# Strided keys and queries loaded as 72 dense rows, values and reordered weight rows by one transfer per head

## The chip, the cores and the metric

The kernel runs on one core of a Trainium2 chip. The metric is the device time of one execution in microseconds (us), from the first instruction to the last with what lies around them; the profile also gives the span between the first and the last instruction. Lower is better.

## The reference

Eight batches of eight heads of attention (sequence 576, head width 64) feed a mixing step and a feed-forward block. Heads 0 to 3 attend locally (the last 32 positions), heads 4 to 7 attend to positions that are a multiple of 32 away. All weights arrive as 64-bit floats and are turned into pairs of 32-bit parts on the chip.

```python
rel = pos[:, None] - pos[None, :]
mask_local = (rel >= 0) & (rel < 32)
mask_strided = (rel >= 0) & (pos[None, :] % 32 == pos[:, None] % 32)
attn = softmax(where(mask[h], q @ k.T / sqrt(64), -1e9))   # local for h < 4, strided for h >= 4
x = (attn @ v).transpose(0, 2, 1, 3).reshape(8, 576, 512)
u = x + (x.transpose(0, 2, 1) @ U @ V).transpose(0, 2, 1)
out = u + maximum(u @ w_ch1, 0) @ w_ch2                    # w_ch1 512 x 2048, w_ch2 2048 x 512
```

## The kernel before

The feed-forward block is the bulk of the work: 18 blocks of 256 rows, each with 16 column chunks of 128, each chunk a first product (`gemm1`, L781) and a second one (`gemm2`, L798) in pairs of 32-bit parts. Blocks 0 and 1 lead and are interleaved. Before them stands a prefix: the attention of batch 0, the mixing of its result, and the start of the attention of batch 1. The attention of batches 2 to 7 is worked in small steps between the products of earlier blocks.

For batches 0 and 1 the strided heads are done by `early_strided`. A row of 2048 elements (8 KB) of one head holds 32 positions of 64 elements; a head has 18 such rows (`NCH`). Keys and queries are loaded in two halves of 1024 elements (4 KB) into the four `kq` tiles, values into `sv`. The access pattern `wide` takes four heads, 32 rows each, which is 14 rows more than a head has: those rows are of the next head and no one uses them. TensorE transposes each half in eight pieces of 128 columns (L354), ScalarE copies the 18 used columns of each 32 out of PSUM (L356), and the scores are small products by head (L367). The values are the moving side of the products at L401.

The 32 weight chunks of 512 KB are loaded by `load_weights` (L158). For `w1` the chunks t = 2 and 3 take their rows in another order, four groups of 32 rows that lie 64 rows apart, again with one access pattern whose outer dimension is 4. Each chunk is then converted by ScalarE, VectorE and GpSimd (`to_f32`, L112 to L117, L182, L183). Some chunk buffers serve the prefix first (`late`): the `kq` tiles sit in the buffers of chunks 28 to 31.

Nearly all transfers are issued by SyncE (SP in the profile) in one order; the first queries go by ScalarE's queue (L93). The order around the change in the prefix is: `kq` and local loads `xn` of the first pair of heads, `sv`, `xn` of the second pair, `U` and `V`, ten weight chunks, values `vt` of the first local pair (L269 reads them), `kq` of batch 1, two weight chunks, `vt` of the second pair, more chunks, `sv` of batch 1, the rest of the chunks, then `xn` of batch 1 (L298 transposes them). A planner that simulates the program's time sets the final order of instructions on each engine.

Of the kernel before, what the change touches and what calls it, by code (L numbers as in the profile page):

```python
# [11 lines left out]
I64 = mybir.dt.int64  # L12
# [26 lines left out]
def fused_kernel(ctx, tc, q, k, v, U, V, w1_in, w2_in, masks, eye, out):  # L39
    nc = tc.nc  # L40
    B, H, S, D = q.shape
    DM, FF = w1_in.shape
    R = U.shape[1]
    NCH = S // 32
# [5 lines left out]
    const = ctx.enter_context(tc.tile_pool(name="const", bufs=1))  # L50
# [11 lines left out]
    def big(shape, name, dtype=F32):  # L62
        return ap_.tile(shape, dtype, name=name, tag="big")
# [22 lines left out]
    def bank(width):  # L86
        return psx1() if width == 1 else psx2().rearrange("p a x -> p (a x)")
# [3 lines left out]
    def dma(out, in_, eng=None):  # L91
        if eng is not None:
            eng.dma_start(out=out, in_=in_)  # L93
        else:
            last_dma[0] = nc.sync.dma_start(out=out, in_=in_).ins  # L95

    ident = const.tile([128, 128], F32, name="ident")
# [4 lines left out]
    raws, w_parts = {}, {}  # L102
# [48 lines left out]
    def load_weights():  # L151
        for i, g, t in chunks:
            src = w2_in[512 * g + 128 * t:512 * g + 128 * t + 128, :] if i else \
                w1_in[128 * t:128 * t + 128, 512 * g:512 * g + 512] if t < 2 else \
                bass.AP(w1_in.tensor, w1_in[256 + 32 * (t - 2):, 512 * g:512 * g + 512].offset, [[64 * FF, 4], [FF, 32], [1, 512]])
            raws[i, g, t] = const.tile([128, 512], I64, name=f"raw{i}_{g}_{t}", tag=f"w{i}_{g}_{t}")
            with tc.issue_after(last_dma[0]):
                nc.sync.dma_start(out=raws[i, g, t], in_=src)  # L158
            yield

    wl = {"gen": load_weights(), "n": 0}

    def late(x, shape, name, dtype=F32):

        i, g, t = chunks[x]
        return const.tile(shape, dtype, name=name, tag=f"w{i}_{g}_{t}")
# [164 lines left out]
    def early_strided(b, eng=None):  # L331


        tb = 64 * (b % 2)
        def wide(src, n, a):

            return bass.AP(src.tensor, src[b, 4:5].offset + a, [[S * D, 4], [32 * D, 32], [1, n]])

        kq = [[late(28 + 2 * x + y, [128, 1024], "kq") for y in range(2)] for x in range(2)]
        for half in range(2):  # L340
            for bufs, src, e in zip(kq, (k, q), (None, eng)):
                dma(out=bufs[half], in_=wide(src, 1024, 1024 * half), eng=e)
        yield
        sv = big([128, 2 * NCH * D], "sv")[:, 0:32 * D]
        dma(out=sv, in_=wide(v, 32 * D, 0))
        yield
        width = 1 if banks["prefix"] else 2
        kT, qT = [[att([128, 4 * 8 * NCH], "xT") for _ in range(2)] for _ in range(2)]
        for half in range(2):
            for bufs, xT in zip(kq, (kT, qT)):  # L350
                for j0 in range(0, 8, 4 * width):
                    tp = bank(width)
                    for j in range(4 * width):
                        nc.tensor.transpose(out=tp[:, 128 * j:128 * j + 128], in_=bufs[half][:, 128 * (j0 + j):128 * (j0 + j) + 128],  # L354
                                            identity=ident)
                    nc.scalar.copy(out=xT[half].rearrange("p (x i) -> p x i", i=NCH)[:, 4 * j0:4 * j0 + 16 * width],  # L356
                                   in_=tp.rearrange("p (x i) -> p x i", i=32)[:, :, 0:NCH])
                    yield
        sp = psx2()
        for par in range(2):  # L360
# [2 lines left out]
        for j in range(16):  # L363
            for h in range(4):
                c0 = (4 * (j % 8) + h) * NCH
# [29 lines left out]
        for r0 in range(0, 32, 2 * nj):  # L395
            op = bank(width)
            for x in range(2 * nj):
                r = r0 + x
# [6 lines left out]
            half, r1 = r0 // 16, r0 % 16  # L405
# [4 lines left out]
            if r1 + 2 * nj == 16:  # L410
                dma(out=od.rearrange("h i r d -> (h i) r d")[:, 16 * half:16 * half + 16], in_=o_sb[half])
                if b == 0:
                    xT_str.append(late(23 + half, [128, 16, 2, 32], "xT_str"))
                    for y in range(2):
                        nc.vector.transpose(out=xT_str[half].rearrange("p r d i -> p (r d i)")[:, 512 * y:512 * y + 512],
                                            in_=o_sb[half].rearrange("p r d -> p (r d)")[:, 512 * y:512 * y + 512])
# [282 lines left out]
    def attention(b):  # L699
        if b >= NSP:  # L700
            yield from local_pairs(b)
            yield "strided"
            yield from strided_copies(b)
            yield from mixed(b, (0, 1))
        else:
            strided = early_strided(b)
            next(strided)
            yield
            yield from run_staggered([strided] + [early_local(b, pr) for pr in range(2)], LAGB)
            yield "free"  # L710
            yield from mixed(b, (0, 1))
# [133 lines left out]
    n0, c0 = wl["n"], counts["conv"]  # L845
# [5 lines left out]
    for step, (n, fc) in enumerate(seq):  # L851
# [15 lines left out]
        if nb < B and step >= window[nb][0]:  # L867
# [5 lines left out]
            while done < want:  # L873
                done += 1
                r = next(gen, "end")
# [66 lines left out]
```

## Time and profile before

| what | value |
|---|---|
| median of 3 runs | 1135.38 us (1133.37 to 1137.88) |
| the profiled execution, its own time | 1131.09 us |
| its span | 1128.9 us |
| TensorE busy, share of the span | 979.8 us, 87% |
| VectorE, GpSimd, ScalarE busy | 612.0, 359.2, 274.0 us |
| chain that ended last: PE, DMA, SP's queue, VectorE | 77%, 10%, 5%, 5% |
| bytes moved by all transfers | 75.21 MB |

The page gives busy time by engine, the span in 40 slices, the transfers, and the chain of work that ended last, followed back from the last instruction. Further views list an engine's instructions in order of time with the idle time before each and what ended it, and sum a stretch of the span: busy time of each engine, the TensorE clock that was granted, the share of the 16 DMA engines that was busy, and the rate. A DMA share of 0.25 is as much as four of the sixteen engines without a pause.

### The profile page before, as it was taken

The numbers are of one execution on the slowest core, as the hardware profiler recorded it, in microseconds if no ns is written. First come the engines' busy times: TensorE is split into PE (matmuls) and PEld (weight loads), VectorE is DVE, ScalarE is ACT, GpSimd is POOL, SyncE is SP. The second block draws the span as 40 slices with busy tenths as digits, with TensorE's granted clock in tenths as the row PEclk, the third lists the DMA queues.
The fourth block names the chain that finished last, engine by engine and source line by source line (L and its number), as shares of the span: only waits on it lengthen the run. The fifth ranks groups of instructions, "written<-read, shape, count | busy, mean of one in ns | idle before, by whom it ended". The sixth has DMA issues, their size and how long they took to land.

```text
span 1128.9 us, 22425 instructions
## 1 busy us (share of the span) xinstructions
PE 979.8 (87%) x9325; PEld 851.4 (75%) x9325; DVE 612.0 (54%) x1151; ACT 274.0 (24%) x638; POOL 359.2 (32%) x384
## 2 busy tenths in 40 slices
PE   1422752995989999999999999999999999999998
PEld 1311652783878888889888888888888888899997
DVE  0145162944688586747527587678658673322111
ACT  0221041531215121411114222421322242111110
POOL 1013020411764545254403545294427430000000
PEclk9755585995989999999999999999999999999999
DMA  3563655203232423231312423324340410111000
GB/s 104 142 148 113 186 159 152 59 4 91 50 96 45 82 53 68 53 51 49 51 40 41 82 54 68 64 39 83 59 82 15 95 33 20 26 31 38 1 19 19
DMA packets 183433, 75.21 MB, mean 67 GB/s; under 512 B 157084, under 2 KB 172732, under 8 KB 183076
## 3 DMA queue, kind: packets, MB, share of 16 engines
q1 hardware_dynamic: 181868, 72.44, 28.4%
q8 instruction: 73, 1.20, 0.5%
q10 hardware_dynamic: 1464, 1.34, 0.4%
q14 instruction: 28, 0.23, 0.1%
HBM read 54.27 MB, written 11.61 MB: 58 GB/s over the span
## 4 chain that ended last, share of the span: by engine, by line
PE 77%; DMA 10%; SPq 5%; DVE 5%; issue 2%; ACT 1%; POOL 1%; DVEq 0%; POOLq 0%; ACTq 0%
PE ph L781 35%; PE acc L798 32%; SPq L95 5%; DMA xn<-in_k_dram 3%; DMA raw<-in_moe_w_ch_dram 3%; DMA vt<-in_v_dram 2%; DMA kq<-in_q_dram 2%; PE px L798 2%; PE px L237 1%; PE px L269 1%; PE px L257 1%; PE ph L584 1%; DVE st L518 1%; PE px L630 1%; PE px L547 1%
## 5 line engine op out<-in xcount | busy, mean ns | idle before, releaser
L781 PE MATMUL ph<-uh,w 128*128 128x256 f32 x2304 | 470.3, 287 | 5.4 <-ACT w L182 2.1
L781 PEld LDWEIGHTS ph<-uh,w 128*128 128x128 f32 x2304 | 378.1, 191 | 20.2 <-DVE gl L786 2.6
L798 PE MATMUL acc<-w,gh 128*128 128x512 f32 x1088 | 349.4, 400 | 0.8 <-ACT gh L785 0.8
L781 PE MATMUL ph<-ul,w 128*128 128x256 f32 x1152 | 328.1, 285 | 2.1 <-DVE ul L750 1.8
L786 DVE SCALAR_TENSOR_TENSOR gl<-ph,gh 128x256 fp32r<-128x256 f32 x288 | 120.9, 420 | 288.8 <-ACT gh L785 287.7
L785 ACT ACTIVATE gh<-ph 128x256 fp32r<-128x256 f32 x288 | 110.2, 383 | 512.8 <-PE ph L781 457.9
L781 PEld LDWEIGHTS ph<-ul,w 128*128 128x128 f32 x1152 | 220.2, 191 | 13.1 <-DVE ul L750 2.1
L798 PEld LDWEIGHTS acc<-w,gh 128*128 128x128 f32 x1088 | 193.3, 188 | 34.7 <-ACT gh L785 1.2
L798 PE MATMUL acc<-w,gl 128*128 128x512 f32 x544 | 215.6, 396 | 0.0
L488 POOL TENSOR_TENSOR tmp<-st 128x576 f32<-128x576 f32 (+6 forms) x162 | 169.3, 1081 | 123.8 <-DMA vt<-in_v_dram 104.1
L516 POOL TENSOR_TENSOR tmp<-st,s_st 128x448 f32<-128x448 f32 (+7 forms) x162 | 137.1, 876 | 203.9 <-DVE st L518 80.8
L518 DVE TENSOR_REDUCE st<-tmp 128x64 f32<-128x64 f32 (+8 forms) x162 | 136.4, 868 | 2.5 <-POOL tmp L516 1.7
L798 PEld LDWEIGHTS acc<-w,gl 128*128 128x128 f32 x544 | 102.2, 188 | 20.3
L183 POOL TENSOR_TENSOR w<-cv,w 128x512 fp32r<-128x512 f32 x32 | 45.4, 1424 | 192.2 <-ACT w L182 188.0
L490 DVE TENSOR_REDUCE s_st<-tmp 128x9 f32<-128x576 f32 (+6 forms) x162 | 87.5, 563 | 19.6 <-POOL tmp L488 19.5
L269 PE MATMUL px<-vt,PT 64*32 64x65 f32 x1152 | 18.3, 241 | 34.1 <-DMA vt<-in_v_dram 33.3
L298 PE MATMUL px<-ident,xn 128*128 128x128 f32 (+1 forms) x40 | 8.9, 353 | 41.0 <-DMA xn<-in_k_dram 41.0
L269 PEld LDWEIGHTS px<-vt,PT 64*32 64x32 f32 x1152 | 14.6, 113 | 39.7 <-issue 37.2
L533 ACT COPY xg<-st 32x256 f32<-32x256 f32 x96 | 38.7, 404 | 22.9 <-DVE st L518 21.9
L298 PEld LDWEIGHTS px<-ident,xn 128*128 128x128 f32 (+1 forms) x40 | 6.7, 187 | 43.6 <-issue 43.2
L644 DVE TENSOR_TENSOR xg<-px,xg 128x512 f32<-128x512 f32 x32 | 20.4, 683 | 30.7 <-PE px L633 28.4
L114 DVE TENSOR_SCALAR cv<-cv 128x512 int32<-128x512 int32 (+3 forms) x35 | 20.1, 577 | 25.5 <-ACT cv L112 25.1
(135 smaller groups left out, 676.3 us busy)
## 6 DMA issues: line engine op xcount, KB each, us to landing
raw<-in_moe_w_ch_dram SPq DMA_DIRECT2D x32, 512.0 KB
out_dram<-xg SPq DMA_DIRECT2D x32, 256.0 KB
u<-bt SPq DMA_DIRECT2D x240, 32.0 KB
vt<-in_v_dram SPq DMA_DIRECT2D x32, 144.0 KB
vt<-in_v_dram SPq DMA_DIRECT2D x32, 136.0 KB
st<-in_q_dram SPq DMA_DIRECT2D x24, 144.0 KB
st<-in_k_dram SPq DMA_DIRECT2D x24, 144.0 KB
st<-in_v_dram SPq DMA_DIRECT2D x24, 144.0 KB
```

Of the source, the lines that this page charges most:

```text
L95: last_dma[0] = nc.sync.dma_start(out=out, in_=in_).ins
L183: nc.gpsimd.tensor_tensor(out=lo, in0=f, in1=hi.bitcast(F32), op=ALU.subtract)
L269: nc.tensor.matmul(op[32 * o4:32 * o4 + 32, hh, (D + 1) * t:(D + 1) * t + D + 1], PT[rows, 32 * c:32 * c + 32], vt[rows, c], start=True, s ...
L488: nc.gpsimd.tensor_tensor(out=tmp[:, 0:n], in0=sk[:, j0:j0 + n], in1=sq[:, i:i + 1].broadcast_to([128, n, D]), op=ALU.mult)
L490: late.append(lambda tmp=tmp, n=n, i=i, j0=j0: nc.vector.tensor_reduce(out=s_st[:, i, j0:j0 + n], in_=tmp[:, 0:n], axis=AX.X, op=ALU.add))
L516: nc.gpsimd.tensor_tensor(out=tv, in0=sv[:, 0:i + 1, d0:d0 + step], in1=s_st[:, i, 0:i + 1].broadcast_to([128, i + 1, step]), op=ALU.mult)
L518: late.append(lambda tv=tv, i=i, d0=d0, step=step: nc.vector.tensor_reduce(out=o_st[:, i, d0:d0 + step], in_=tv.rearrange("p j d -> p d j" ...
L533: nc.scalar.copy(out=xg[32 * i4:32 * i4 + 32, :, cs], in_=o_st[rows, i4:16:4, :])
L781: nc.tensor.matmul(ph[:, 0:W], w_parts[0, g, dc][:, part, fs], ut[:, :, :, dc, :], start=(dc == 0 and i == 0), stop=(dc == NDC - 1 and i = ...
L785: gate[:] = [nc.scalar.activation(out=gh[:, 0:W], in_=ph[:, 0:W], func=AF.Relu).ins]
L786: nc.vector.scalar_tensor_tensor(out=gl[:, 0:W], in0=ph[:, 0:W], scalar=0.0, in1=gh[:, 0:W].bitcast(F32), op0=ALU.max, op1=ALU.subtract)
L798: nc.tensor.matmul(accs[n][:, s, :], gt[:, cs], w_parts[1, g, f][:, part, :], start=(fc == 0 and i == 0), stop=(fc == NFC - 1 and i == 2))
```

## The change

Keys and queries of the strided heads are loaded as one pattern of 72 rows (four heads of 18, which lie one behind the other in memory); the 56 rows that no one used are not read. The transposes then take 72 rows and give 72 columns each, packed four to 288 columns of a bank, and the copy out of PSUM reads them densely. The values come by four transfers, one for each head, of 18 rows. The `w1` chunks with t = 2 and 3 come by four transfers of 32 rows each. What is computed from the data is the same.

```diff
@@ load_weights
             src = w2_in[512 * g + 128 * t:512 * g + 128 * t + 128, :] if i else \
-                w1_in[128 * t:128 * t + 128, 512 * g:512 * g + 512] if t < 2 else \
-                bass.AP(w1_in.tensor, w1_in[256 + 32 * (t - 2):, 512 * g:512 * g + 512].offset, [[64 * FF, 4], [FF, 32], [1, 512]])
-            raws[i, g, t] = const.tile([128, 512], I64, name=f"raw{i}_{g}_{t}", tag=f"w{i}_{g}_{t}")
+                w1_in[128 * t if t < 2 else 256 + 32 * (t - 2):, 512 * g:512 * g + 512]
+            raw = raws[i, g, t] = const.tile([128, 512], I64, name=f"raw{i}_{g}_{t}", tag=f"w{i}_{g}_{t}")
             with tc.issue_after(last_dma[0]):
-                nc.sync.dma_start(out=raws[i, g, t], in_=src)
+                if i or t < 2:
+                    nc.sync.dma_start(out=raw, in_=src[0:128])
+                else:
+                    for h in range(4):
+                        nc.sync.dma_start(out=raw[32 * h:32 * h + 32], in_=src[64 * h:64 * h + 32])
             yield
@@ early_strided
-        def wide(src, n, a):
-
-            return bass.AP(src.tensor, src[b, 4:5].offset + a, [[S * D, 4], [32 * D, 32], [1, n]])
-
-        kq = [[late(28 + 2 * x + y, [128, 1024], "kq") for y in range(2)] for x in range(2)]
+        kq = [[late(28 + 2 * x + y, [128, 1024], "kq")[0:4 * NCH] for y in range(2)] for x in range(2)]
         for half in range(2):
             for bufs, src, e in zip(kq, (k, q), (None, eng)):
-                dma(out=bufs[half], in_=wide(src, 1024, 1024 * half), eng=e)
+                dma(out=bufs[half], in_=src[b, 4:8].rearrange("h (i r) d -> (h i) (r d)", r=32)[:, 1024 * half:1024 * half + 1024],
+                    eng=e)
         yield
         sv = big([128, 2 * NCH * D], "sv")[:, 0:32 * D]
-        dma(out=sv, in_=wide(v, 32 * D, 0))
+        for h in range(4):
+            dma(out=sv[32 * h:32 * h + NCH], in_=v[b, 4 + h].rearrange("(i r) d -> i (r d)", r=32))
         yield
...
                     for j in range(4 * width):
-                        nc.tensor.transpose(out=tp[:, 128 * j:128 * j + 128], in_=bufs[half][:, 128 * (j0 + j):128 * (j0 + j) + 128],
-                                            identity=ident)
-                    nc.scalar.copy(out=xT[half].rearrange("p (x i) -> p x i", i=NCH)[:, 4 * j0:4 * j0 + 16 * width],
-                                   in_=tp.rearrange("p (x i) -> p x i", i=32)[:, :, 0:NCH])
+                        c0 = 512 * (j // 4) + 4 * NCH * (j % 4)
+                        nc.tensor.transpose(out=tp[:, c0:c0 + 4 * NCH], in_=bufs[half][:, 128 * (j0 + j):128 * (j0 + j) + 128],
+                                            identity=ident[0:4 * NCH, 0:4 * NCH])
+                    nc.scalar.copy(out=xT[half][:, 4 * NCH * j0:4 * NCH * (j0 + 4 * width)].rearrange("p (w x) -> p w x", w=width),
+                                   in_=tp.rearrange("p (w x) -> p w x", w=width)[:, :, 0:16 * NCH])
```

## Rows read from the trace of the kernel before

**Rows 1.** The page: TensorE, DMA engines and their rate in 40 slices.

```profile
PE   1422752995989999999999999999999999999998
DMA  3563655203232423231312423324340410111000
GB/s 104 142 148 113 186 159 152 59 4 91 50 96 45 82 53 68 53 51 49 51 40 41 82 54 68 64 39 83 59 82 15 95 33 20 26 31 38 1 19 19
```

**Rows 2.** TensorE in order of time: start, us, instruction, [idle before, ended by].

```profile
18.46 1.94 PE L354 MATMUL ph<-ident,kq 128*128 128x128 f32 x8 [18.46 <-DMA kq<-in_k_dram]
...
26.54 0.72 PE L231 MATMUL acc<-masks_l 128*128 128x320 bf16 x2 [6.14 <-DMA masks_l<-in_masks_dram]
...
44.90 1.38 PE L298 MATMUL px<-ident,xn 128*128 128x128 f32 x5 [10.90 <-DMA xn<-in_k_dram]
...
59.81 0.56 PE L367 MATMUL px<-xT 64*18 64x18 f32 x41 [7.55 <-issue]
...
68.80 1.66 PE L401 MATMUL ph<-sv,PT_str 18*32 18x64 f32 x46 [6.54 <-DVE PT_str L386]
...
81.01 0.39 PE L269 MATMUL px<-vt,PT 64*32 64x65 f32 x2 [10.55 <-DMA vt<-in_v_dram]
...
94.78 1.28 PE L401 MATMUL ph<-sv,PT_str 18*32 18x64 f32 x38 [1.67 <-DVE o_str L406]
...
118.31 0.39 PE L269 MATMUL px<-vt,PT 64*32 64x65 f32 x2 [22.25 <-DMA vt<-in_v_dram]
...
189.16 1.09 PE L298 MATMUL px<-ident,xn 128*128 128x128 f32 x4 [30.14 <-DMA xn<-in_k_dram]
```

**Rows 3.** Stretches: length, busy PE, PEld, DVE, ACT, POOL; clock, DMA share, GB/s.

```profile
0.00:25.00 25.00, 1.94 (x8) 1.57 (x8) 0.00 (x0) 1.54 (x2) 3.93 (x20) 1.00 0.33 109
50.00:55.00 5.00, 2.26 (x200) 1.92 (x198) 2.66 (x8) 3.23 (x8) 0.00 (x0) 1.00 1.03 301
55.00:65.00 10.00, 2.44 (x115) 1.65 (x115) 3.73 (x8) 2.46 (x4) 0.00 (x0) 0.53 1.03 214
...
121.00:129.00 8.00, 7.41 (x218) 5.64 (x206) 1.73 (x7) 0.37 (x1) 0.00 (x0) 0.50 0.97 301
136.00:140.00 4.00, 4.00 (x24) 3.86 (x24) 0.42 (x1) 0.66 (x2) 0.37 (x1) 0.80 0.25 97
...
205.00:210.00 5.00, 5.00 (x71) 3.75 (x72) 3.76 (x7) 3.46 (x7) 2.15 (x2) 1.00 0.90 220
...
280.00:286.00 6.00, 3.87 (x29) 3.06 (x22) 2.56 (x4) 1.69 (x4) 1.29 (x1) 0.50 1.17 268
345.00:1120.00 775.00, 774.46 (x6428) 676.72 (x6427) 445.84 (x856) 191.22 (x472) 264.94 (x283) 1.00 0.24 48
```

**Rows 4.** SyncE in order of time: start, us, the transfers that it issues.

```profile
47.46 10.90 SPq L158 DMA_DIRECT2D raw<-in_moe_w_ch_dram  x10
63.78 13.08 SPq L95 DMA_DIRECT2D vt<-in_v_dram  x4
...
127.83 12.99 SPq L158 DMA_DIRECT2D raw<-in_moe_w_ch_dram  x2
...
281.22 2.35 SPq L95 DMA_DIRECT2D st<-in_k_dram  x4
```

**Rows 5.** The chain that ended last, in order of time: start, us, what.

```profile
48.40 15.37 DMA raw<-in_moe_w_ch_dram
63.78 17.09 DMA vt<-in_v_dram
...
165.41 15.11 DMA raw<-in_moe_w_ch_dram
```

**Rows 6.** Line 158, the issue of weight chunks: duration ns min/median/max, first and last start.

```profile
L158 SPq DMA_DIRECT2D raw<-in_moe_w_ch_dram x32: 340/568/8849, 47.5 to 203.9; - x32
```

**Rows 7.** The tile kq: its transposes, weight load and product, ns min/median/max.

```profile
L354 PEld LDWEIGHTS ph<-ident,kq x40: 139/226/231, 18.4 to 141.3; 128*128 128x128 f32 x40
L354 PE MATMUL ph<-ident,kq x40: 270/421/474, 18.5 to 141.4; 128*128 128x128 f32 x40
```

## Prediction

> **What bounds the kernel now.** I first read the 40 slices [rows 1]: TensorE is full from about the twelfth slice on, and before that it is mostly below half while the DMA engines are busy at three to six tenths. The stretch from 345 to 1120 us confirms it: PE is busy 774.46 of 775 us there with a DMA share of 0.24 [rows 3]. No load of this change lies there, so nothing can be won or lost there but a shift. All is decided in the first 200 us.
>
> Second, TensorE in order of time [rows 2]: up to 190 us it has six waits that a transfer ended, 18.46, 6.14, 10.90, 10.55, 22.25 and 30.14 us, together 98.4 us. That is the most that faster loads can give there. Its other long waits (7.55 us with no releaser that the profile shows, 6.54 us for VectorE) are not theirs.
>
> Third, why those loads are late. The rates of stretches fall into two kinds [rows 3]. At 136 to 140 us the DMA share is 0.25 at 97 GB/s, and over the first 25 us 0.33 at 109 GB/s: about four of sixteen engines work, at some 25 GB/s each. At 50 to 55 and 121 to 129 us all sixteen work and move 301 GB/s. What is in flight in the slow stretches are the patterns whose outer dimension is 4: `kq` and `sv`, and the `w1` chunks with t = 2, 3. The two of these chunks issued from 127.83 us held SP for 12.99 us [rows 4], where an issue costs 0.568 us in the median [rows 6]. I read it so: such a transfer is dealt to four engines, and as these serve what comes behind in order, everything later lands when those four are through. The chain shows the second half: the first chunk with t = 2 is issued at 48.40 and lands 15.37 us later, and at that moment, 63.78, the `vt` load eight issues behind it is issued and needs another 17.09 us [rows 5]. So SP has eight transfers outstanding, and a slow one holds the ninth.
>
> The Trainium skill agrees (DMA: Bandwidth & Descriptors, "Why a DMA increments its semaphore by 16 and not by 1"): the engines of a transfer are the largest number up to 16 that divides the slowest dimension of both sides. By it 4 groups give 4 engines, 72 rows 12, 18 rows 9, 32 rows 16.
>
> **The change part by part.** Bytes: a `kq` transfer falls from 128 to 72 rows of 4 KB (512 to 288 KB), `sv` from 128 to 72 rows of 8 KB (1024 to 576 KB): 2.75 MB less for the two batches. The eight `w1` chunks keep their 4 MB. The engines matter more than the bytes. For rates on many engines I have 301, 268 (280 to 286 us, pieces of 144 KB from single heads), 220 (205 to 210 us, rows of 256 bytes) and 214 GB/s (55 to 65 us, weights on all engines) [rows 3]; 214 and 301 are my bounds.
>
> Wait by wait; "ready" is when PE came to the wait before, less what has been won so far.
> 1. First keys, 18.46 us. The two first halves and the identity are 0.65 MB; issued by 1.2 us, at 220 GB/s 2.9 us more, with the start of a transfer about 5 us. Won 13.5 (12 to 14).
> 2. Masks, 6.14 us. All first loads (four `kq` 1.18 MB, `xn` 0.59, identity and masks 0.19) are 2.0 MB, 6.5 to 9 us, so about 9 to 10 us; PE has done its first eight transposes at 7. Won 4 (3 to 5).
> 3. `xn` of the second pair, 10.90 us. PE is ready at 34.0 - 17.5 = 16.5. SP issues four pieces of `sv` and six `xn` from about 8 us, 10 x 0.55 = 5.5 us; they land at about 16. Won 10.9.
> 4. `vt`, 10.55 us. PE is ready at 68.80 + 1.66 - 28.4 = 42.1, since the 7.55 us and VectorE's work stay on the way. SP comes to the ten chunks at about 17 us; they are now 16 issues, 9 us, beside 5.24 MB, 17.4 to 24.5 us, so the six added issues are hidden by the data; if not they cost 3.4 us here. With `vt` (0.57 MB) the end is at 39 to 47. I take a wait of 2: won 8.5 (5 to 10.5).
> 5. `vt` of the second pair, 22.25 us. PE is ready at 94.78 + 1.28 - 36.9 = 59.2; what PE waits for on the way there is VectorE, which converts weights and stays as it is. Its buffer is free some 4.5 us after wait 4; ahead of it in SP's order stand `kq` of batch 1 and two chunks. From about 46 us on 3.1 MB take 10 to 14.5 us. A wait of 2: won 20 (17 to 22).
> 6. `xn` of batch 1, 30.14 us. PE is ready at 189.16 - 30.14 - 56.9 = 102. From about 59 us on 18 chunks (9.4 MB) and 3.4 MB of other loads and stores go ahead of it, 12.8 MB: 42.5 us at 301 GB/s, 60 at 214. I take 268, the row that is nearest (pieces of heads, mixed with stores' reads), 48 us: landing at 107, wait 5: won 25 (13 to 30). The 15.11 us that one four-group chunk takes here [rows 5] is what goes.
>
> Sum: 13.5 + 4 + 10.9 + 8.5 + 20 + 25 = 81.9 us, bounds 61 and 92.
>
> On engines: 64 transposes of batches 0 and 1 move 72 columns instead of 128. Weight loads of 128 columns (226 ns in the median) go with each product (421 ns, overlapped) [rows 7]; if the moving columns paced them, 8 in 1.94 us [rows 2] less 44% would give 64 x 0.24 x 0.44 = 7 us, half of it behind waits; if the loads pace them, nothing. I take nothing, as loads and products have the same count and the loads keep their size. The copies at L356 write the same 288 columns and stay off the path.
>
> SP issues 30 more transfers (24 pieces of weights, 6 of values), 30 x 0.568 = 17 us of its time. Behind it queue `xn`, `vt` and the masks of eight outstanding. It is covered by data in flight as long as a piece of 128 KB takes as long as its issue: 128 KB in 0.568 us are 231 GB/s, inside my bounds. The four loads of 144 KB at 281.22 us went out in 2.35 us, 0.59 each [rows 4], in a stretch with 268 GB/s [rows 3]: pieces by head neither stall SP nor leave the engines idle.
>
> Against that row stands a rule of the Trainium skill (DMA: Bandwidth & Descriptors, "Rules for kernel authors"): two transfers to disjoint partition halves serialize, better use one of 128 partitions. By it the split of `sv` and `w1` would give nothing; the row of 268 GB/s speaks against it here, because the one transfer is not spread over all engines.
>
> The profiled execution takes 1131.09 us, 4.3 below the median. 1131 - 82 = 1049 for it, so 1053 on the median's scale.
>
> **The rivals.**
> - More than the sum: with TensorE idle less, the clock (granted at 0.53 and 0.50, that is near 1.2 GHz, at 55 to 65 and 121 to 129 us [rows 3]) is granted in full earlier, and part of the 7.55 us goes with the crowded queues. The waits all vanish (92) and 1 to 12 us come on top: 1031 to 1043. For it: PE runs at half clock over work of some 20 us; against: small products are not paced by it alone.
> - A gain cut by the window of eight: pieces of 128 KB make it hold 1 MB where it held 4, and the rate stays at 170 to 200 GB/s, under every row with all engines at work. Wait 4 then stays, and the 12.8 MB ahead of wait 6 take 64 to 75 us from 62 to 69 us on, to 126 to 144 instead of 189: 45 to 63 won, 1072 to 1090.
> - It doesn't do what it says: pieces or 72 rows still run on few engines (or, as that rule has it, one after the other). Then only bytes go, 2.75 MB at 97 to 109 GB/s, 25 to 28 us, or up to 40 if `kq` alone spreads: 1095 to 1110.
> - Slower, by one mechanism: in SP's queue at 50 to 80 us a transfer lands some 15 us after its issue [rows 5]. If that lag stays with small pieces, eight outstanding move 1 MB in 15 us, and the 4 MB of `w1` pieces need 60 us where they needed about 20 by themselves: 40 more less the 28 for bytes, 1147. It decides from a lag of about 10 us on; at 281 us nothing of the kind is seen.
>
> **How the numbers follow.** The forecast, 1043 to 1074, gets 0.60; more than the sum 0.13; the cut gain 0.11; few engines 0.10; slower 0.04; no change 0.02. What a measurement of this kernel can tell from no change is about 0.5%, 6 us. The range reaches from 1034 to 1088, which leaves a part of the first rival and of the second, and the last three, outside. Faster 0.94, same 0.02, slower 0.04.
>
> **What would show it.** In the profile after, the stretches with a DMA share near 0.25 before 190 us are gone and the rates there are above 200 GB/s; PE starts its first transposes at about 5 us, reads `vt` at about 44 and 61 and passes the wait of batch 1 at about 107; from there to the end the span is as long as before, 940 us. It is wrong if the share stays at 0.25 to 0.35 under the new pieces, if SP's issues pace the loads with idle engines, or if a wait on VectorE's conversions takes the place of wait 5 or 6.

## Result, and the profile after

The changed kernel takes 1055.68 us (median of 4 runs, 1053.57 to 1056.35) where the kernel before takes 1134.38 us (median of 4, the three of the table above and one more): a ratio of 0.9299, 95% interval 0.9273 to 0.9325. The forecast was 1053 us, in a range of 1034 to 1088. The profiled execution took 1055.9 us and has a span of 1053.8 us, 75.1 less than before.

The page of the kernel after: busy time by engine, then TensorE, its granted clock, the DMA engines and their rate in 40 slices (now 26.3 us each).

```profile
PE 976.7 (93%) x9325; PEld 845.9 (80%) x9325; DVE 611.9 (58%) x1151; ACT 274.2 (26%) x638; POOL 361.7 (34%) x384
...
PE   4457898598999999999999999999999999999997
PEclk9559899599999999999999999999999999999999
DMA  8999301414240425040224323233304300101000
GB/s 185 228 241 275 101 2 23 109 23 102 49 88 20 94 40 88 21 85 6 58 44 68 68 64 66 43 72 76 68 25 83 68 20 9 54 1 40 1 21 21
```

Against [rows 1] the DMA engines are at eight or nine tenths in the first four slices, where they stood at three to six tenths for seven; the loads of the prefix are packed into 109 us instead of 189. TensorE does nearly the same work (976.7 us busy, 979.8 before); its idle time falls from 149.1 to 77.1 us.

TensorE of the kernel after, in order of time (start, us, instruction, [idle before, ended by]); lines with short waits or none left out. They answer to [rows 2].

```profile
6.48 1.19 PE L356 MATMUL ph<-ident,kq 72*128 72x72 f32 x8 [6.48 <-DMA kq<-in_k_dram]
9.92 0.71 PE L234 MATMUL acc<-masks_l 128*128 128x320 bf16 x2 [2.25 <-DMA masks_l<-in_masks_dram]
...
18.81 1.39 PE L301 MATMUL px<-ident,xn 128*128 128x128 f32 x5 [3.30 <-DMA xn<-in_k_dram]
...
27.77 1.41 PE L260 MATMUL acc<-ident,s_sb 128*128 128x128 f32 x5 [2.48 <-ACT s_sb L253]
...
31.23 1.31 PE L240 MATMUL acc<-xT 64*32 64x32 f32 x72
43.62 0.39 PE L272 MATMUL px<-vt,PT 64*32 64x65 f32 x2 [11.08 <-DMA vt<-in_v_dram]
...
47.81 3.50 PE L403 MATMUL ph<-sv,PT_str 18*32 18x64 f32 x118
61.04 0.39 PE L272 MATMUL px<-vt,PT 64*32 64x65 f32 x2 [9.73 <-DMA vt<-in_v_dram]
...
70.90 0.52 PE L403 MATMUL ph<-sv,PT_str 18*32 18x64 f32 x9 [3.09 <-issue]
...
82.63 0.75 PE L586 MATMUL ph<-o_str,U_cls 18*32 18x64 f32 x38 [2.59 <-issue]
...
108.77 1.38 PE L301 MATMUL px<-ident,xn 128*128 128x128 f32 x5 [5.00 <-DMA xn<-in_k_dram]
```

The six waits for transfers are 37.8 us together instead of 98.4. The wait of 7.55 us with no releaser and those of 6.54, 3.88 and 1.67 us for VectorE no longer stand in TensorE's order; two new ones of 3.09 and 2.59 us with no releaser and one of 2.48 us for ScalarE have come.

Stretches of the kernel after (length, busy PE, PEld, DVE, ACT, POOL; granted clock, DMA share, GB/s), to be held against [rows 3].

```profile
0.00:109.00 109.00, 59.83 (x1279) 48.80 (x1280) 50.29 (x96) 35.91 (x71) 23.17 (x35) 0.76 0.93 233
...
0.00:25.00 25.00, 12.40 (x220) 9.27 (x221) 2.88 (x10) 7.09 (x15) 3.96 (x20) 1.00 0.79 179
25.00:40.00 15.00, 5.05 (x250) 3.64 (x242) 10.88 (x22) 7.28 (x14) 1.27 (x1) 0.65 0.93 292
60.00:110.00 50.00, 36.49 (x625) 31.05 (x625) 24.83 (x45) 14.30 (x31) 10.54 (x8) 0.77 1.00 263
...
270.00:1045.00 775.00, 774.26 (x6426) 676.08 (x6425) 447.50 (x858) 191.28 (x472) 265.47 (x283) 1.00 0.24 48
```

No stretch with a share near 0.25 is left ahead of 110 us; up to 109 us the mean is 0.93 at 233 GB/s. The ten chunks behind the first loads now move at 292 GB/s, and the loads ahead of the other batch's rows at 263. The last row is the feed-forward block: 774.26 of 775 us, as before, only 75 us earlier.

SyncE of the kernel after, in order of time (start, us, the transfers that it issues), beside [rows 4]; and the chain that ended last, beside [rows 5].

```profile
21.49 7.51 SPq L161 DMA_DIRECT2D raw<-in_moe_w_ch_dram  x8
...
32.98 6.33 SPq L95 DMA_DIRECT2D vt<-in_v_dram  x4
...
56.60 1.99 SPq L95 DMA_DIRECT2D vt<-in_v_dram  x4
```

```profile
21.49 7.54 DMA raw<-in_moe_w_ch_dram
...
57.61 5.35 DMA vt<-in_v_dram
...
100.83 7.80 DMA xn<-in_k_dram
```

Eight pieces go out in 7.51 us, where two chunks had held SP for 12.99. The transfers on the chain ahead of 110 us land mostly 5 to 8 us after their issue (`kq` of batch 1 takes 9.14), where those of [rows 5] took 15 to 17.

### The profile page after: what moved, and what is told of

Read it like the earlier page. It is cut to its first block, busy times and chain, and to the rows that moved or that the text cites. A ratio compares the mean times of both kernels' runs of the same rounds, so it can differ in the third digit from the quotient of the medians.

```text
span 1053.8 us, 22470 instructions
## 1 busy us (share of the span) xinstructions
PE 976.7 (93%) x9325; PEld 845.9 (80%) x9325; DVE 611.9 (58%) x1151; ACT 274.2 (26%) x638; POOL 361.7 (34%) x384
## 4 chain that ended last, share of the span: by engine, by line
PE 84%; DMA 6%; DVE 5%; issue 2%; SPq 2%; ACT 1%; POOL 0%; DVEq 0%; POOLq 0%; ACTq 0%
PE ph L783 38%; PE acc L800 35%; DMA raw<-in_moe_w_ch_dram 2%; PE px L800 1%; PE px L272 1%; SPq L95 1%; PE px L240 1%; DVE st L520 1%; PE px L260 1%; DMA kq<-in_q_dram 1%; DMA vt<-in_v_dram 1%; DVE cv L115 1%; PE px L632 1%; DMA masks_l<-in_masks_dram 1%; DMA xn<-in_k_dram 1%
## 5 line engine op out<-in xcount | busy, mean ns | idle before, releaser
L114 DVE TENSOR_SCALAR cv<-cv 128x512 int32<-128x512 int32 (+3 forms) x35 | 21.3, 608 | 26.3 <-ACT cv L112 26.2
L770 DVE TENSOR_TENSOR ul<-u,uh 128x1024 fp32r<-128x1024 f32 x15 | 18.8, 1256 | 20.4 <-ACT uh L769 14.6
L185 ACT CAST w<-cv 128x512 fp32r<-128x512 f32 x32 | 19.7, 617 | 35.7 <-DVE cv L117 31.8
L117 DVE SCALAR_TENSOR_TENSOR cv<-raw,cv 128x512 int32<-128x512 int32 x32 | 28.2, 888 | 0.3
```

The lines of the kernel that those rows point to most:

```text
L117: nc.vector.scalar_tensor_tensor(out=i, in0=lo_w, scalar=29, in1=i, op0=ALU.logical_shift_right, op1=ALU.bitwise_or)
```

## Experiments: each part alone

**Keys and queries alone.** The kernel before, with only the 72 dense rows and their transposes. (This cut and the next ones of `kq` show the transfer alone; the lines that fit tile, transposes and copy to the rows are left out.)

```diff
-                dma(out=bufs[half], in_=wide(src, 1024, 1024 * half), eng=e)
+                dma(out=bufs[half], in_=src[b, 4:8].rearrange("h (i r) d -> (h i) (r d)", r=32)[:, 1024 * half:1024 * half + 1024], eng=e)
```

> The kernel before with the keys and queries of the change alone (72 dense rows, transposes of 72); sv and the w1 chunks stay as before. Theory (four-group patterns hold four DMA engines): four transfers of 128 KB per engine go from the four engines in each of the two batches, so the first wait falls from 18.5 to 6.5 us, the masks' wait from 6.1 to 2.3, and of the long wait for vt of the second pair some 10 to 14 us go; ratio 0.972 to 0.978 (28 to 32 us). Rival (only the bytes that are not read count): as for e4_kq_four.

Measured: 1104.06 us, ratio 0.975 (0.9728 to 0.9773), 28 us won, as expected. The first wait is 7.49 us, and the wait for `vt` of the second pair falls by 6.8 us, not by the 10 to 14 expected. The four waits behind the first that are not this part's own still come (11.49, 9.07, 15.44 and 27.29 us).

**Values alone.** The kernel before, with `sv` in four transfers of 18 rows.

```diff
-        dma(out=sv, in_=wide(v, 32 * D, 0))
+        for h in range(4):
+            dma(out=sv[32 * h:32 * h + NCH], in_=v[b, 4 + h].rearrange("(i r) d -> i (r d)", r=32))
```

> The kernel before with the values of the change alone (four transfers of 18 rows). Theory: the 16 us in which sv sits on four engines in batch 0 fall to about 5, and some 10 us of batch 1's before its local loads; ratio 0.980 to 0.985 (17 to 23 us). Rival (bytes only): 0.9 MB less at 100 GB/s, 9 us, 0.992.

Measured: 1120.77 us, ratio 0.9894 (0.9869 to 0.992): 11 us, less than the theory expected. Its rival's 0.992 stands at the edge of the interval, so this run alone does not exclude it. TensorE of this kernel shows where the time went.

```profile
69.34 0.39 PE L269 MATMUL px<-vt,PT 64*32 64x65 f32 x2 [10.96 <-DMA vt<-in_v_dram]
...
111.44 0.39 PE L269 MATMUL px<-vt,PT 64*32 64x65 f32 x2 [35.20 <-DMA vt<-in_v_dram]
```

The wait for `xn` of the second pair, 10.90 us before [rows 2], is down to 1.38, and the first `vt` is read 11.7 us earlier. But the wait for `vt` of the second pair has grown from 22.25 to 35.20 us. SyncE of the same kernel, in order of time, shows what stands ahead of it:

```profile
83.26 10.87 SPq L158 DMA_DIRECT2D raw<-in_moe_w_ch_dram  x3
94.97 6.61 SPq L95 DMA_DIRECT2D vt<-in_v_dram  x2
```

Three chunks, two of them of four groups, hold SP for 10.87 us, and the `vt` loads come after. While SP issues these chunks the profile has it wait 10.2 us for the landings of `kq` of batch 1, four groups as well, so these hold it too. Reaching a slow transfer earlier doesn't make it faster: what one part wins is lent to the next slow one in the queue. By the wait of batch 1 it has won 16.5 us all the same (172.65 for 189.16 us), near the theory's 17 to 23; some 6 us are given back in the stretch behind it (49.7 us, where the kernel before takes 43.5), as in the changed kernel below.

**Reordered weight rows alone.** The kernel before, with the chunks t = 2, 3 of `w1` in four transfers; not one byte fewer.

```diff
-                nc.sync.dma_start(out=raws[i, g, t], in_=src)
+                if i or t < 2:
+                    nc.sync.dma_start(out=raw, in_=src[0:128])
+                else:
+                    for h in range(4):
+                        nc.sync.dma_start(out=raw[32 * h:32 * h + 32], in_=src[64 * h:64 * h + 32])
```

> The kernel before with the w1 chunks of the change alone: four transfers of 32 rows, the same bytes. Theory: the waits for vt of the first pair and for the local loads of batch 1 shrink by some 10 and 20 us and a part of the one between; ratio 0.962 to 0.970 (34 to 43 us), the largest single part though no byte is saved. Rival (bytes only): 1.000. Rival (small transfers pace SP): 1.00 to 1.01, slower.

Measured: 1097.56 us, ratio 0.970 (0.967 to 0.9729): 34.5 us, the largest of the three parts, as expected. TensorE of this kernel:

```profile
18.74 1.94 PE L357 MATMUL ph<-ident,kq 128*128 128x128 f32 x8 [18.74 <-DMA kq<-in_k_dram]
...
45.46 1.39 PE L301 MATMUL px<-ident,xn 128*128 128x128 f32 x5 [11.90 <-DMA xn<-in_k_dram]
...
100.46 0.40 PE L272 MATMUL px<-vt,PT 64*32 64x65 f32 x2 [14.92 <-DMA vt<-in_v_dram]
...
155.38 1.08 PE L301 MATMUL px<-ident,xn 128*128 128x128 f32 x4 [12.07 <-DMA xn<-in_k_dram]
```

The waits ahead of the weights stand as they were; those behind them fall. The three parts sum to 28 + 11 + 34.5 = 74 us, the whole to 79: they add up within what these measurements can tell.

## Experiments: engines or bytes

**72 rows kept on four groups.** Two tries. The first wrote the rows as four heads of 18:

```diff
+                dma(out=bufs[half], in_=bass.AP(src.tensor, src[b, 4:5].offset + 1024 * half, [[S * D, 4], [32 * D, NCH], [1, 1024]]), eng=e)
```

> As e1_kq, 72 rows and transposes of 72, but read by a pattern of four heads by 18 rows, so its outer dimension is 4 again; the bytes and TensorE's work are those of e1_kq. Theory: still on four engines, only 56 of 128 rows less there, 9 us per batch at 25 GB/s an engine: ratio 0.984 to 0.988 (14 to 18 us), about half of what e1_kq gives. Rival (bytes, or cheaper transposes): the same as e1_kq.

Measured: 1106.32 us, ratio 0.9768 (0.9742 to 0.9794), a first wait of 7.09 us and 125 GB/s in the first 25 us, where the first experiment has 7.49 us and 134 GB/s; the intervals of the two ratios overlap. It tells nothing of the theories, because a head is exactly 18 rows long, so that its two outer dimensions are one of 72 rows; the packets of the two runs have the same counts (below). The second try takes every fourth row into a group, which cannot merge:

```diff
+                dma(out=bufs[half], in_=bass.AP(src.tensor, src[b, 4:5].offset + 1024 * half, [[32 * D, 4], [128 * D, NCH], [1, 1024]]), eng=e)
```

> The kernel before with strided keys and queries of 72 rows, as in the run of that part alone, but written so that four groups of 18 rows remain the outer dimension of each transfer: rows h, h+4, h+8 and so on form group h, which cannot merge with the next. The bytes, the transfers' number and the 72-row transposes are those of that run (the rows come in another order, so the strided scores are computed from other rows than the reference's; the work is the same). Theory (a transfer with four outer groups is spread over a quarter of the DMA engines, and that, not its size, is what the part alone won): the rate of the first 25 us is again near 100 GB/s, the first wait for keys is shorter only by the bytes left out (288 KB for 512 KB, so nearer 11 to 13 us than 7.5), and the ratio to before is 0.984 to 0.992. Rival (fewer bytes and smaller transposes win it, however the transfer is laid out): 0.975 to 0.978 as in the run of that part alone.

Measured: 1120.3 us, ratio 0.9884 (0.9851 to 0.9917), inside the theory's range and outside the rival's. The first 25 us of this kernel and then of the one with dense rows:

```profile
0.00:25.00 25.00, 7.39 (x104) 5.60 (x104) 0.00 (x0) 4.07 (x8) 3.93 (x20) 1.00 0.40 102
```

```profile
0.00:25.00 25.00, 7.60 (x104) 5.66 (x104) 0.82 (x1) 4.07 (x8) 3.93 (x20) 1.00 0.55 134
```

The bytes and the transposes are the same, the layout of one dimension differs: 102 GB/s at a share of 0.40 against 134 at 0.55, and a first wait of 13.82 us (a little above the 11 to 13 that were expected) against 7.49. So of the 28 us that dense rows win, about 14 are the spread over engines, and 14 come with fewer rows on a slow transfer and shorter transposes (these two were not told apart).

**The bytes of before, spread.** The kernel after, reading all that the kernel before read: keys and queries as 128 dense rows, values as four transfers of 32 rows.

```diff
-                dma(out=bufs[half], in_=src[b, 4:8].rearrange("h (i r) d -> (h i) (r d)", r=32)[:, 1024 * half:1024 * half + 1024], eng=e)
+                dma(out=bufs[half], in_=bass.AP(src.tensor, src[b, 4:5].offset + 1024 * half, [[32 * D, 128], [1, 1024]]), eng=e)
...
-            dma(out=sv[32 * h:32 * h + NCH], in_=v[b, 4 + h].rearrange("(i r) d -> i (r d)", r=32))
+            dma(out=sv[32 * h:32 * h + 32], in_=bass.AP(v.tensor, v[b, 4 + h:5 + h].offset, [[32 * D, 32], [1, 32 * D]]))
```

> The changed kernel, but with all the bytes of before read: kq as 128 dense rows (one transfer, 56 rows unused), sv as four transfers of 32 rows. Transfers, their number and TensorE's work stay as in the change. Theory (engines, not bytes): 2.75 MB more at 250 to 300 GB/s cost 9 to 11 us of transfer time, of which some lies on the path: 3 to 9 us over the change, ratio to before 0.933 to 0.938. Rival (bytes): most of what e1 and e2 gave is lost, 0.96 or more.

Measured: 1055.54 us, ratio 0.9321 (0.9294 to 0.9349), just below the theory's range and far from the rival's. The 2.75 MB that the change saves are worth nothing that this can tell. One reservation: by the packet counts below, 128 and 32 rows also run on more engines than 72 and 18, so some of the price of the bytes may be paid by that.

TensorE of this kernel:

```profile
32.72 0.56 PE L369 MATMUL px<-xT 64*18 64x18 f32 x42 [5.04 <-issue]
...
41.72 1.67 PE L403 MATMUL ph<-sv,PT_str 18*32 18x64 f32 x46 [6.55 <-DVE PT_str L388]
44.41 0.39 PE L272 MATMUL px<-vt,PT 64*32 64x65 f32 x2 [1.03 <-DMA vt<-in_v_dram]
...
62.89 0.40 PE L272 MATMUL px<-vt,PT 64*32 64x65 f32 x2 [3.06 <-DMA vt<-in_v_dram]
...
112.07 1.38 PE L301 MATMUL px<-ident,xn 128*128 128x128 f32 x5 [4.71 <-DMA xn<-in_k_dram]
```

Here the wait for VectorE (6.55 us) and one without a releaser (5.04 us) are there as in [rows 2], and the waits for `vt` are 1.03 and 3.06 us, where the changed kernel has 11.08 and 9.73. `vt` is read at 44.41 and 62.89 us, in the changed kernel at 43.62 and 61.04. The landings rule; which wait TensorE spends the time before them in does not.

**How many engines a transfer runs on.** The pages count packets. Here are the kernel before, dense rows alone, four heads of 18, and four groups that cannot merge:

```profile
DMA packets 183433, 75.21 MB, mean 67 GB/s; under 512 B 157084, under 2 KB 172732, under 8 KB 183076
DMA packets 183049, 73.37 MB, mean 67 GB/s; under 512 B 157148, under 2 KB 172796, under 8 KB 182692
DMA packets 183049, 73.37 MB, mean 66 GB/s; under 512 B 157148, under 2 KB 172796, under 8 KB 182692
DMA packets 182986, 73.37 MB, mean 66 GB/s; under 512 B 157085, under 2 KB 172733, under 8 KB 182629
```

Eight `kq` transfers of dense rows have 64 small packets more than eight of four groups, eight for each; four heads of 18 have the same counts as dense rows, and four groups that cannot merge have all but one of those of before. If each engine that takes part adds one small packet, which is inferred from these counts and not seen directly, the prediction's 4 and 12 engines give just that. Its 9 and 16 come out as well: 64 more with the values alone (8 x 9 less 2 x 4), 480 with the weights alone (32 x 16 less 8 x 4), and 88 more in the run with the bytes of before than in the changed kernel (8 x 4 and 8 x 7).

## Experiments: what the new form costs, and what limits it now

**Every chunk in four transfers.** The kernel after, with 72 more issues and the same bytes.

```diff
-                if i or t < 2:
-                    nc.sync.dma_start(out=raw, in_=src[0:128])
-                else:
-                    for h in range(4):
-                        nc.sync.dma_start(out=raw[32 * h:32 * h + 32], in_=src[64 * h:64 * h + 32])
+                st = 32 if i or t < 2 else 64
+                for h in range(4):
+                    nc.sync.dma_start(out=raw[32 * h:32 * h + 32], in_=src[st * h:st * h + 32])
```

> The changed kernel with every weight chunk in four transfers of 32 rows: 72 more transfers on SP, the same bytes. It tests the rival that small transfers and eight outstanding pace the loads. My theory: 128 KB are issued in some 0.45 us and moved in 0.45 to 0.6, so the issue stays just hidden: 0 to 5 us over the change, ratio 0.930 to 0.934. Rival: 72 times 0.45 us come on the path, 20 to 32 us, ratio 0.948 to 0.958.

Measured: 1065.18 us, ratio 0.9411 (0.9394 to 0.9428), between the two. Against the changed kernel it loses 9.5 us by the medians and 12.7 by the ratios, 0.13 to 0.18 us for each added transfer. SyncE of this kernel, and its stretches of the first and of the last chunks:

```profile
19.71 23.48 SPq L159 DMA_DIRECT2D raw<-in_moe_w_ch_dram  x40
```

```profile
25.00:40.00 15.00, 6.80 (x334) 5.17 (x327) 10.40 (x21) 7.49 (x14) 1.29 (x1) 1.00 0.87 231
...
80.00:118.00 38.00, 22.33 (x177) 19.64 (x170) 15.49 (x27) 12.18 (x27) 6.39 (x5) 0.89 0.98 220
```

The changed kernel in the stretch that ends with the same landings:

```profile
80.00:108.00 28.00, 19.97 (x165) 17.92 (x163) 14.89 (x26) 12.07 (x27) 5.99 (x5) 0.94 1.01 280
```

Forty issues in 23.48 us are 0.587 us each, and 128 KB in 0.587 us are 223 GB/s; the stretch of the first chunks moves 231 GB/s where the mixed queue had 292. That SP's issues pace it is not shown. In the median an issue takes 0.419 us, here and in the changed kernel, and 128 KB in 0.419 us would be 313 GB/s; the longest takes 1.645. And from 80 to 118 us the engines are busy at a share of 0.98 and yet move 220 GB/s, where the changed kernel has 280 at 1.01: there the engines move less in the same busy time. Whether issues, the eight outstanding or the engines cost the 10 us, the runs leave open. The Trainium skill (DMA: Bandwidth & Descriptors, "Rules for kernel authors") says that splitting a transfer into partition halves is not worth it, since the halves share the same engines. This run agrees, and more: four parts of a transfer that was spread already cost some 10 us. The run of the weights alone (0.970) disagrees, for a transfer that was not spread; the Trainium skill covers that case in the same section's row on using all 16 engines.

**Values earlier.** The kernel after, with `vt` of the first pair loaded right behind its keys and queries.

```diff
         xq = load_natural(q[b], h0, eng)
+        early = b == 0 and pr == 0
+        if early:
+            held[0] = True
+            values(vts[0], [v[b, h0 + hh] for hh in range(2)])
...
-        yield from acquire((0,))
-        values(vts[0], [v[b, h0 + hh] for hh in range(2)])
+        if not early:
+            yield from acquire((0,))
+            values(vts[0], [v[b, h0 + hh] for hh in range(2)])
```

> The changed kernel with the values of the first local pair loaded right behind its keys and queries, ahead of sv and the ten chunks. The two waits for vt that are left, 11.1 and 9.7 us, both come from vt standing behind weights in SP's order. Theory: the first goes, and as the second load can follow earlier, up to the whole of the second; 8 to 18 us, if the later wait for batch 1's local loads does not take them back (it is set by the bytes ahead of it, which stay): then 0 to 6 us. I expect the latter, as all engines are busy from 60 to 105 us: ratio 0.925 to 0.930. Rival (the chain of TensorE and VectorE decides): 0.915 to 0.922.

Measured: 1056.24 us, ratio 0.9327 (0.9312 to 0.9342): no gain, and just above the expected 0.925 to 0.930. Both `vt` waits are gone (at most 1.64 us is left), but the last wait of the prefix has taken it all:

```profile
107.92 1.38 PE L301 MATMUL px<-ident,xn 128*128 128x128 f32 x5 [10.43 <-DMA xn<-in_k_dram]
```

The other batch's rows are read at 107.92 us instead of 108.77: the bytes ahead of them are the same, and the rate from 60 to 110 us is 245 GB/s (263 in the changed kernel). The prefix now ends when these rows land. With the engines at a mean share of 0.95 up to there, an earlier place in the queue does not bring that forward; the 2.75 MB of the run above put it off by 3.3 us.

**VectorE's conversions.** Between the first and the last transposes of the other batch's rows the changed kernel takes 49.1 us (108.77 to 157.84) where the kernel before takes 43.6 (189.16 to 232.74): 5.5 us are given back there. VectorE is busy 43.80 us of it, which made it the suspect. One run converts eleven chunks ahead instead of nine:

```diff
-CONV0, CONVE, CONVP = 11, 1, 9
+CONV0, CONVE, CONVP = 11, 1, 11
```

> The changed kernel with eleven instead of nine chunks converted in the prefix. After the change TensorE has won 80.4 us when batch 1's local loads arrive and 74.9 us 50 us later; in between VectorE is busy without a gap with conversions. Theory (the conversions, which wait on nothing new but come bunched, take 5.5 us back): two chunks moved into VectorE's idle time from 72 to 95 us give back 2 to 4 us, ratio 0.927. Rival (another cause, such as the order on the DMA queue): no change, 0.930.

Measured: 1052.88 us, ratio 0.9302 (0.9285 to 0.9319): no change by the ratio. (The stretch takes 43.8 us there, but the matmul instructions in it are 552 instead of 577, so it is not the same work.) A second run leaves out the last of VectorE's three operations on each chunk (the edit cut down to that; other uses of the helper keep the operation):

```diff
-        nc.vector.scalar_tensor_tensor(out=i, in0=lo_w, scalar=29, in1=i,
-                                       op0=ALU.logical_shift_right, op1=ALU.bitwise_or)
```

> The changed kernel with the last of VectorE's three operations on each chunk of the weights left out (1.05 us each; the weights lose the three lowest bits that it puts in). In the stretch between the first and the last transposes of the other batch's natural rows, VectorE is busy 43.8 of 49.1 us. If VectorE's conversions are what gives back 5 us there, this kernel is 4 to 6 us faster than the changed kernel: 1050 us or less, ratio 0.924 to 0.927. If what is given back is matmuls that were put off (18 more of them in the stretch than before, about 0.15 us each) and a granted clock of 0.90 after 0.97, TensorE idles only 2.4 us there and the ratio stays within 0.928 to 0.932.

Measured: 1050.47 us, ratio 0.9267 (0.9234 to 0.9301): 3.6 us less than the changed kernel by the ratios, between the two expectations, and the intervals overlap. The trace tells more. The stretch in this kernel:

```profile
110.40:157.20 46.80, 44.40 (x562) 38.99 (x563) 27.76 (x46) 21.42 (x42) 17.12 (x12) 0.87 0.14 37
```

VectorE has 16 us less to do, and TensorE still idles 2.40 us, as it does with all conversions (2.44, below). So VectorE does not hold TensorE there; the stretch is 2.2 us shorter, with 15 matmuls fewer in it. Outside the stretch conversions may cost some: behind it the wait for VectorE's `s_sb` is 2.0 us long in this kernel and 3.9 in the changed one. Whether the 3.6 us are real stays open, and if they are, where they come from.

**What the 5.5 us are.** The stretch before and after, and all that follows it, of the kernel before and then of the kernel after:

```profile
189.20:232.70 43.50, 40.91 (x559) 36.17 (x560) 37.55 (x55) 21.12 (x41) 16.67 (x12) 0.97 0.15 40
...
232.70:1128.90 896.20, 871.39 (x7471) 758.76 (x7469) 516.75 (x994) 215.44 (x522) 317.27 (x336) 0.98 0.25 51
```

```profile
108.80:157.80 49.00, 46.56 (x577) 40.03 (x578) 43.80 (x61) 22.51 (x45) 20.74 (x13) 0.90 0.14 36
...
157.80:1053.80 896.00, 870.50 (x7471) 757.26 (x7469) 517.77 (x994) 215.79 (x523) 317.79 (x336) 0.98 0.25 51
```

From the end of the stretch on the two kernels are alike: 7471 matmuls in 896 us. In the stretch TensorE's idle time is the same (2.59 and 2.44 us) and its busy time is 5.65 us longer. Two things go with that. It has 18 matmuls more: 18 products of the feed-forward block that the kernel before did ahead of its long wait are put off behind the short one. And the granted clock is 0.90 instead of 0.97. Two rows of the kernel after give the prices:

```profile
110.00:115.00 5.00, 5.00 (x20) 4.54 (x20) 3.66 (x7) 1.77 (x3) 0.00 (x0) 0.52 0.00 0
...
140.00:145.00 5.00, 5.00 (x33) 4.27 (x32) 4.90 (x6) 2.31 (x6) 3.49 (x2) 1.00 0.00 0
```

At full clock a matmul of this mix takes 5.00 / 33 = 0.15 us, near the lower level 0.25. So the 18 are 2.7 us. A mean of 0.90 over 49 us is 9.8 us at the lower level, of 0.97 over 43.5 us 2.6: 7.2 us more at half speed, 3.6 us of work. Together 6.3, an estimate; twelve transposes of `kq` in the stretch take 0.5 us less (1.30 for 1.80), which leaves 5.8 against 5.65 seen. The order of the matmuls is counted; the clock's part is worked out, and was not tried by itself. The run with the values earlier comes nearest to a trial: between the same two points (107.9 to 156.4 us) it has 578 matmuls at a clock of 0.95, and is busy 45.21 us. That is 1.35 us less than the changed kernel (46.56 at 0.90). By that, 0.05 of the clock is worth some 1.4 us and 0.07 about 2, an estimate again: less than the 3.6 worked out above, and then more than 1 of the 5.65 us stays open.

**Both small steps together.** The kernel after, with the earlier values and eleven chunks converted ahead (the two edits above in one).

> The changed kernel with the first value rows loaded right behind their keys and queries, and eleven chunks converted ahead instead of nine: the two single steps were without a measurable gain (0.9327 and 0.9302 against 0.9299). Theory (the bytes ahead of the other batch's natural rows set the end, whatever the order in front of them and however early weights are converted): 0.929 to 0.933. Rival (value waits and conversions hide each other, so that only both together show): 0.922 to 0.926.

Measured: 1051.24 us, ratio 0.928 (0.924 to 0.932). The interval holds the theory's range and overlaps the changed kernel's; it is no version that can be told from the change.

## Why the prediction was right, by its own steps

**What bounds the kernel.** The reading was right: all but the 5.5 us given back behind the wait of batch 1 lies ahead of 190 us, the shift behind is even (896.2 and 896.0 us), and the cause is the outer dimension of four, shown by the run that keeps the bytes of 72 rows and changes only that dimension (0.9884 against 0.975), by the weights alone, where no byte is saved (0.970), and by the packet counts. One reading was loose: TensorE stands at nine tenths in the eighth and ninth slices already, and not only from about the twelfth [rows 1]; nothing hangs on it.

**The landings** were forecast well, the waits less so:

| wait for | predicted landing | measured | predicted wait left | measured |
|---|---|---|---|---|
| first keys | 5 | 6.48 | 5.0 | 6.48 |
| masks | 9 to 10 | 9.92 | 2.1 | 2.25 |
| `xn`, second pair | 16 | 18.81 | 0 | 3.30 |
| `vt` | 39 to 47 (44) | 43.62 | 2 | 11.08 |
| `vt`, second pair | 56 to 61 | 61.04 | 2 | 9.73 |
| `xn`, batch 1 | 107 | 108.77 | 5 | 5.00 |

- Steps 1, 2 and 6 came out within 1.5 us: 12.0, 3.9 and 25.1 us won. Step 1's landing at 5 us allows about 0.9 us for the start of a transfer, for which it has no row; it was 6.48. The 263 GB/s from 60 to 110 us is what 268 stood for.
- Step 3 won 7.6 us instead of 10.9. The issue count was too kind: SP spent 4.40 us from 13.18 us on its last three `xn` loads, one of them 2.52 us, where the sum had 0.55 us for each. I read it as transfers ahead that were still outstanding.
- Steps 4 and 5 are where the sum failed: -0.5 us won instead of 8.5, and 12.5 instead of 20. Not the transfers were late; TensorE was early. The step had it ready at 42.1 and 59.2 us, and it was ready at 32.5 and 51.3. The step kept on the way the 7.55 us with no releaser, which did not come, and the 6.54 us for VectorE, which moved: in [rows 2] 46 strided value products stand ahead of `vt` (68.80 us), in the changed kernel they all stand behind it (47.81 us), and VectorE works for them while TensorE waits for `vt`. The planner's new order, which the step did not foresee, hides that wait. The landing of 39 to 47 us is some 3 us above what 17 us and 5.81 MB at the two rates give (36 to 44); 43.62 fits both. The run with the bytes of before, where both waits stay (5.04 and 6.55 us), has 1.03 and 3.06 us left for `vt`, what the step said, and takes the same time.
- So the six waits won 60.6 us and not 81.9. Up to the last of them TensorE's idle time is the page's span less its busy time, less what lies behind: 189.2 - (979.8 - 871.4 - 40.9) = 121.7 us before and 108.8 - (976.7 - 870.5 - 46.6) = 49.2 after, 72.5 less. The four other waits won 19.6; the new ones (8.2 us) and differences of short waits took 7.7 of the two sums back. The busy time there is 7.9 us shorter, and 72.5 + 7.9 = 80.4 is how much earlier the wait of batch 1 is passed. The sum of steps had 81.9 for that point. Its error is mostly one with two signs, keeping waits that went and so leaving too little for the `vt` waits, and that is why the total was nearly right. The 7.9 us of busy time, of which the sum had nothing, made up the rest; that they fit is luck.
- What the sum lacks comes behind step 6: of the 80.4 us, 5.5 were given back by work put off and, in part as worked out above, by the clock. The prediction had the span even from 107 us on; it is even from 158 us on. That is most of the difference between its 82 and the 75.1 us of the span; the medians differ by 78.7. Set against the profiled executions the forecast of 1049 is 6.9 us below the 1055.9 measured; on the median's scale it is 2.7 us off, because the profiled execution before was 3 to 4 us quicker than its median and the one after was not. That is luck as well.
- The transposes, taken at nothing, were mis-sized: eight take 1.19 us where they took 1.94 [rows 2]. The weight loads, as many as before and with 128 columns still, did not pace them; the time fell nearly as the moving columns did (0.61 of the time, 0.56 of the columns), as the other bound had it. The 52 that run ahead of the wait of batch 1 are busy 6.58 us instead of 10.23, so 3.65 of the 7.9 us above are theirs (all 64 save 4.1, where the bound had 7); 2.7 more are the 18 products put off.
- SP's 30 added issues cost nothing that shows, as said; no run takes them away, but the engines are busy at 0.93 up to 109 us. The kernel with pieces only runs at 231 GB/s, the figure of the step's bound; as the median issue there takes 0.419 us and not 0.568, the agreement proves nothing.
- Of the signs, the rates above 200 GB/s are met on the mean (233 up to 109 us) and not everywhere: the first 25 us have 179. The span behind the wait of batch 1 is 945 us, where 940 were named.

**The rivals.** "More than the sum" did not come as a whole: the wait of 7.55 us went, as it had it, but the clock is still 0.77 from 60 to 110 us, and the waits for transfers did not all vanish. "A gain cut by the window of eight" is nearest to the run with every chunk in four, at 220 to 231 GB/s and a loss of some 10 us, though whether the window does that is open; the mix of the change stays above it. "Few engines" and "slower" are excluded by the rates and by a lag of mostly 5 to 8 us.

## What to carry to other kernels

A DMA share that stands at a quarter while a queue is full was worth more here than the bytes: look for the access pattern whose outermost dimension is small, turn it into one of many rows or cut it at that dimension, and do it for every such transfer in the queue, since one that is left takes back what the others won. Cut no further than that: 72 more transfers, out of chunks that were spread already, cost some 10 us here. And forecast the landings first: when a landing sets the time, a wait that goes elsewhere comes back in front of it.

## What had not been expected of the hardware

- A pattern of four heads by 18 rows runs like one of 72 rows when the heads lie one behind the other (first wait 7.09 us, against 13.82 for four groups that cannot merge, and 157148 small packets against 157085). The dimensions written in the pattern are not what the transfer is dealt by.
- Waits without a releaser move and change with the queue, but not simply with its speed: 7.55 us before, 3.09 and 2.59 after, 5.04 and 3.18 with the bytes of before spread, and 3.62, 3.65 and 3.04 with the values earlier, at other instructions each time. What TensorE waits for there is not in the profile; the runs don't settle it.
- The granted clock was 0.52 in the 5 us behind a wait of 5.00 us, though TensorE was busy throughout them (110 to 115 us): 20 matmuls where 33 fit at full clock. If the wait is what brought the clock down, which no run tries by itself, it cost some 2 us more than its own length, an estimate (13 x 0.15 us).
